# Exact weights alone out of the first stage, late turns by heads, and another order

## The chip, the core and the metric

The kernel runs on one NeuronCore of a Trainium2 chip. The metric is the device time of one execution in microseconds (us). Before the change the median of three runs is 785.89 us (785.5 to 787.57). Five engines run side by side, each through its own list of instructions: TensorE (PE in the rows) multiplies, VectorE (DVE) and ScalarE (ACT) do elementwise work, GpSimd (POOL) adds integers, SyncE (SP) issues transfers. An instruction starts when the one ahead of it on its engine is through and the semaphores of its operands allow it.

## The reference

```
scores = q_c @ k_c.T / 8           # 8 batches x 8 heads, chunks of 64 tokens, width 64
attn = exp(scores - max) ; attn = attn / (sum(attn) + 1e-09)
x = attn @ v_c                     # as 4608 tokens x 512
h = x @ w_in                       # 512 x 2048, float64 words
g = s * relu(h)**2 + b
out = g @ w_out                    # 2048 x 512, float64 words
```

## The kernel before

Every product of two fp32 matrices is made of three TensorE products: each operand is split into a high part (a cast on ScalarE) and a low part (the difference, on VectorE), and h·h, h·l and l·h are added up in PSUM. All large matmuls have 512 columns.

Tokens go in blocks of 512 and more. The *first stage* (tokens 0 to 511) is plain: its `up` products (L657), relu, square, split of g into `g_hi` (L674) and `g_lo` (L678), and `down` products (L632). Meanwhile it makes the weights. They come as 64-bit words in 16 "pairs" of tiles, k = 0 to 15, and each pair goes through a chain: `load` on SP, `tail` (L176) and `scale` (L172) on ScalarE, `shift` (L182) and `sign` (L184) on VectorE, `add` (L190) on GpSimd, `hi` (L194) on ScalarE, `lo` (L198) on VectorE. Attention for the tokens runs beside it in groups one, two, ... of 256 tokens: `scores`, `peak` (L373), `sub` (L378), `exp`, `sum` (L387), `normz` (L390, L391), `norm` (L394), then P is transposed on TensorE (`transposes`, L404) and copied by ScalarE (`copies`, L417), or, for groups seven and later, on VectorE (`turn`, L412), and then `values` (L424) and `x_out` (L440).

From *block 0* on, the MLP works with seven products in place of eight for each 2x2 set of tiles (p1 to p7, L713), for which sums of weight quarters are needed: `s_add` (four additions or subtractions, L233), `s_hi` (L238), `s_lo` (L241) for w_in, and `OutSums` for w_out in block 0's second half (the down steps d0 to d31). The high and low parts of all weights and sums are stored in DRAM scratch (w_in, w_out, w_sum) and read again, 1 MB at a time, by `stream.load` (L330, the "ring" steps) into the three buffers of the pool `raw`.

The order of all instructions is written out by hand. The string ORDER names the steps; they are run in that order, and each engine's list follows from it, since the pool of tiles and the scheduler move nothing (`manual_schedule`). Before the change ORDER ends with block 0's first half; block 0's second half is in `direct` and in hooks, the later blocks in loops of their own.

```
for name in ORDER.split():
    named[name.split("/")[0]]()
block.direct()
```

GpSimd does nothing but the adds of the pairs and ends with the last of them, at 116.5 us.

Of the kernel before, what the change touches and what calls it, by code (L numbers as in the profile page):

```python
# [19 lines left out]
one.load_qk0 one.load_qk1 load0b one.load_v load0a two.load_qk0 two.load_qk1 load1 two.load_v three.load_qk one.scores0 one.peak0  # L20
s_and_b sb one.sub0 one.exp0 one.scores1 keep_busy7 one.peak1 one.sum0 three.load_v one.sub1 one.normz0 one.norm0
one.exp1 four.load_v tail0b one.transposes0 keep_busy3 one.sum1 one.normz1 one.copies0 one.norm1 tail0a scale0a load2
one.transposes1 four.load_qk shift0a scale0b two.scores0 keep_busy8 one.copies1 sign0a shift0b add0a two.peak0 two.sub0
hi0a sign0b two.scores1 two.exp0 lo0a add0b two.peak1 one.values0 keep_busy7 two.sum0 one.x_hi0 two.sub1
load3 hi0b one.x_lo0 two.exp1 lo0b one.values1 keep_busy4 tail1 two.normz0 in0 two.sum1 one.x_hi1
scale1 two.norm0 two.normz1 two.transposes0 keep_busy2 two.norm1 one.x_lo1 shift1 two.copies0 two.values0 sign1 two.transposes1
two.x_hi0 two.copies1 add1 two.x_lo0 up1a scale2 tail2 two.values1 shift2 up0a hi1 sign2
two.x_hi1 three.scores lo1 add2 two.x_lo1 in1 three.peak scale3 up1b tail3 three.sub up0b
open_o load4 relu1 shift3 hi2 up3 sign3 relu0 three.exp lo2 square0 square1
add3 three.sum out0 up2 g_hi0 relu3 g_hi1 load5 square3 three.normz tail4 g_lo0  # L30
g_hi3 three.norm down0 scale4 g_lo1 hi3 shift4 relu2 g_lo3 three.transposes sign4 square2
g_hi2 down1 load6 lo3 tail5 scale5 add4 g_lo2 in2 three.copies up4 shift5
hi4 sign5 tail6 load7 four.scores lo4 relu4 scale6 add5 up5 out1 four.peak
square4 five.load_qk g_hi4 four.sub hi5 shift6 down2 load8 g_lo4 relu5 sign6 tail7
scale7 lo5 three.values four.exp add6 in3 square5 up6 four.sum three.x_out g_hi5 shift7
hi6 g_lo5 down3 sign7 relu6 square6 four.normz g_hi6 load9 add7 tail8 g_lo6
up7 scale8 four.norm hi7 lo7 four.transposes relu7 square7 load10 shift8 up8 scale9
in4 lo6 four.copies sign8 g_hi7 tail9 down4 shift9 out2 add8 g_lo7 relu8
square8 tail10 up9 g_hi8 sign9 load11 hi8 g_lo8 add9 scale10 down5 relu9
square9 g_hi9 shift10 hi9 lo8 five.scores sign10 out3 down6 scale11 load12 five.peak  # L40
six.load_qk add10 tail11 g_lo9 five.sub down7 hi10 shift11 lo9 five.exp sign11 in5
four.values lo10 tail12 up11 add11 five.sum scale12 load13 five.load_v out4 four.x_out five.normz
hi11 up10 shift12 five.norm x21.hi relu11 sign12 x11.hi down8 x21.lo relu10 square11
# [6 lines left out]
s_add0 ring2 s_hi1 lo15 s_hi0 s_add7 relu15 six.transposes out7 square15 down13 g_hi15  # L50
s_add5 six.copies s_lo0 six.values s_lo1 s_keep0 g_lo15 down14 six.x_out s_add6 s_keep1 x22.hi
xt1.add_dve seven.scores x22.lo xt1.hi seven.load_v down15 xt3.add_dve eight.load_qk xt1.lo xt3.hi xt2.add_dve p1.0
st2 st1 xt3.lo xt2.hi p2.0 seven.peak u1.0 st0 p1.1 xt2.lo st3 c11.0
p5.0 u1.1 xt4.add_dve relux.0 p6.1 s_add3 xt4.hi p6.0 u2.1 seven.sub p7.1 xt4.lo
ring3 u2.0 seven.exp s_add2 p7.0 u3.1 p2.1 seven.sum u3.0 c22.0 p4.0 seven.normz
c11.1 p3.0 s_add4 c21.0 relux.1 sqx.0 p4.1 ring4 c12.0 seven.norm s_hi2 p1.2
c21.1 s_lo2 split0.hi p5.1 seven.turn0 s_keep2 u1.2 sqx.1 p6.2 reluy.0 c22.1 p2.2
split0.lo u2.2 ring5 sqy.0 seven.turn1 p3.1 split1.hi p7.2 c11.2 s_hi3 seven.turn2 relux.2
p1.3 ring6 u3.2 c12.1 p4.2 seven.turn3 reluy.1 p5.2 u1.3 sqy.1 s_lo3 seven.values
eight.scores ring7 c21.2 c22.2 sqx.2 s_keep3 split1.lo p3.2 seven.x_out eight.peak eight.load_v nine.load_qk  # L60
p2.3 eight.sub s_hi4 c12.2 p6.3 eight.exp c11.3 reluy.2 eight.sum p5.3 ring8 relux.3
s_lo4 sqy.2 p1.4 eight.normz u2.3 s_keep4 eight.norm p2.4 u1.4 eight.turn0 p6.4 p7.3
c11.4 u2.4 eight.turn1 relux.4 p7.4 u3.3 c22.3 p4.3 u3.4 eight.turn2 p3.3 ring9
c21.3 sqx.3 eight.turn3 p1.5 s_hi5 c12.3 p4.4 ring10 s_lo5 u1.5 reluy.3 p5.4
s_keep5 c21.4 sqy.3 eight.values nine.scores c22.4 sqx.4 p3.4 eight.x_out nine.load_v nine.peak p6.5
nine.sub s_hi6 ring11 c12.4 p2.5 nine.exp s_lo6 reluy.4 p1.6 c11.5 ten.load_qk s_keep6
u2.5 nine.sum relux.5 p7.5 sqy.4 nine.normz u1.6 p5.5 nine.norm u3.5 nine.turn0 p4.5
ring12 p2.6 c21.5 c22.5 sqx.5 nine.turn1 p3.5 c11.6 p1.7 s_hi7 c12.5 nine.turn2
relux.6 p6.6 u1.7 reluy.5 p5.6 s_lo7 ring13 u2.6 sqy.5 nine.turn3 p7.6 s_keep7
p6.7 u3.6 c22.6 ring14 p4.6 u2.7 p3.6 c21.6 sqx.6 p2.7 c12.6 reluy.6  # L70
p7.7 c11.7 sqy.6 ring15 p5.7 relux.7 u3.7 d0 c22.7 p3.7 p4.7 c12.7
reluy.7 ring16 c21.7 sqy.7 sqx.7
# [4 lines left out]
def local_attention_then_squared_relu_mlp(ctx: ExitStack, tc, qkv, w, s, b, out):  # L77
# [219 lines left out]
    class Stream:  # L297


        def __init__(self, blocks):  # L300
# [8 lines left out]
            whole = (slice(None),)  # L309
            self.left = [[(t, whole)] for t in (once + direct * 2 + (once + parts) * (blocks - 1))]  # L310
            self.start = [0] + [len(once) + 2 * len(direct) + n * (len(once) + len(parts)) for n in range(blocks - 1)]
            kept = {n for (p, name), n in units.items() if not name.startswith("s")}
            for n in range(7 * NP // 4):
                mine = [u for u in range(4) if 4 * n + u in kept]
                runs = [(u, next(v for v in range(u, 5) if v not in mine)) for u in mine if u - 1 not in mine]
                self.left[n] = [(w_in[:, n, :, u:v], (slice(None), slice(None), slice(u, v))) for u, v in runs]
# [912 lines left out]
```

## Time and profile before

| | |
|---|---|
| median of three runs | 785.89 us |
| span of the profiled execution, first to last instruction | 783.3 us |
| TensorE busy | 770.7 us (98%) |
| VectorE busy | 615.1 us (79%), 891 instructions |
| ScalarE busy | 470.3 us (60%) |
| GpSimd busy | 48.8 us (6%), 23 instructions |
| HBM read, written | 159.38 MB, 44.04 MB |
| TensorE's granted clock over the span | full |

The page gives the profiled execution by its span; the runs' times count what lies around it too, and their median is 2.6 us above it. TensorE sets the time where it never waits, which is read from its idle time by stretch and not from the 98%. The other engines' shares are means over stages that differ: VectorE is all but full up to 150 us and has time to spare behind.

### The profile page before, as it was taken

What the parts mean: (1) busy time and instruction counts of PE and PEld (TensorE: products, weight loads), DVE (VectorE), ACT (ScalarE), POOL (GpSimd) and SP (SyncE); (2) the same over time, 40 slices, a digit from 0 to 9 for tenths busy, and PEclk for the clock granted to TensorE, in tenths of its full rate; (3) what the DMA queues carried; (4) which work ended last, traced back from release to release, by engine and by line L of the source; (5) the groups of instructions that cost most, each with busy time, mean ns of one, the idle gap of its engine ahead of it and who ended that gap; (6) DMA issues with size and microseconds to landing.
All of it is one profiled execution on the core that took longest, in us unless ns stands there. A gap on an engine that the chain in (4) does not pass through costs nothing.

```text
span 783.3 us, 13870 instructions
## 1 busy us (share of the span) xinstructions
PE 770.7 (98%) x5584; PEld 637.7 (81%) x5584; DVE 615.1 (79%) x891; ACT 470.3 (60%) x645; POOL 48.8 (6%) x23
## 2 busy tenths in 40 slices
PE   6899999999999999999999999999999999999998
PEld 5788888888888888888888888888888888888886
DVE  6989899998479986888899858888998723348773
ACT  4899876867643433566864635666846346575442
POOL 1453440000000000000000000000000000000000
PEclk9999999999999999999999999999999999999999
DMA  9999999678568999966466587665565778876653
GB/s 356 354 357 340 365 304 322 224 243 282 178 216 295 327 343 320 335 246 241 165 213 223 181 311 282 253 264 203 168 230 177 242 263 294 300 266 215 209 193 136
DMA packets 79844, 204.33 MB, mean 261 GB/s; under 512 B 5796, under 2 KB 39076, under 8 KB 68516
## 3 DMA queue, kind: packets, MB, share of 16 engines
q1 hardware_dynamic: 79488, 203.18, 74.6%
q8 instruction: 44, 0.72, 0.4%
q10 hardware_dynamic: 292, 0.26, 0.1%
q14 instruction: 20, 0.16, 0.1%
HBM read 159.38 MB, written 44.04 MB: 260 GB/s over the span
## 4 chain that ended last, share of the span: by engine, by line
PE 91%; DMA 4%; ACT 2%; DVE 1%; issue 1%; SPq 0%; ACTq 0%
PE ps_h L713 22%; PE ps_h L933 17%; PE ps_o L713 17%; PE ps_x L933 8%; PE ps_x L632 8%; PE ps_o L632 5%; PE ps_o L933 4%; PE ps_h L657 3%; PE ps_h L632 3%; DMA raw<-in_w_dram 3%; PE ps_a L368 2%; PE ps_x L424 1%; DMA t<-in_qkv_dram 1%; PE ps_a L424 1%; ACT raw L176 1%; ACT t L172 1%
## 5 line engine op out<-in xcount | busy, mean ns | idle before, releaser
L713 PE MATMUL ps_h<-t,raw 128*128 128x512 f32 x672 | 167.3, 391 | 0.0
L713 PEld LDWEIGHTS ps_h<-t,raw 128*128 128x128 f32 x672 | 125.4, 188 | 26.5 <-ACT u L723 0.2
L933 PE MATMUL ps_h<-t,raw 128*128 128x512 f32 (+1 forms) x588 | 142.4, 385 | 0.0
L907 DVE TENSOR_TENSOR t<-t 128x512 fp32r<-128x512 f32 (+1 forms) x120 | 105.2, 896 | 33.3 <-ACT t L905 33.2
L933 PEld LDWEIGHTS ps_h<-t,raw 128*128 128x128 f32 x588 | 108.8, 188 | 22.2
L732 DVE TENSOR_TENSOR t<-ps_o,u 128x512 f32<-128x512 f32 x96 | 66.0, 689 | 75.3 <-PE ps_o L713 69.9
L713 PE MATMUL ps_o<-t,raw 128*128 128x512 f32 x480 | 121.8, 389 | 0.0
L713 PEld LDWEIGHTS ps_o<-t,raw 128*128 128x128 f32 x480 | 90.1, 188 | 18.8
L723 ACT COPY u<-ps_h 128x512 f32<-128x512 f32 x96 | 56.1, 586 | 69.6 <-PE ps_h L713 68.6
L905 ACT CAST t<-t 128x512 fp32r<-128x512 f32 (+1 forms) x120 | 87.3, 788 | 2.8 <-PE ps_h L933 1.9
L412 DVE STREAM_TRANSPOSE pT<-p 32x256 f32<-32x256 f32 x192 | 83.7, 436 | 3.2
L933 PE MATMUL ps_x<-t,raw 128*128 128x512 f32 x288 | 73.1, 389 | 0.0
L776 ACT ACTIVATE t<-t 128x1024 f32<-128x1024 f32 x64 | 67.1, 1052 | 0.2
L933 PEld LDWEIGHTS ps_x<-t,raw 128*128 128x128 f32 x288 | 54.1, 188 | 11.2
L772 ACT ACTIVATE t<-t 128x512 f32<-128x512 f32 (+1 forms) x64 | 54.1, 846 | 10.2 <-DVE t L732 9.7
L190 POOL TENSOR_TENSOR t<-t,raw 128x1024 int32<-128x1024 int32 (+1 forms) x17 | 48.1, 2827 | 67.1 <-DVE t L184 46.4
L632 PE MATMUL ps_x<-t,raw 128*128 128x512 f32 x192 | 48.8, 390 | 0.0
L657 PE MATMUL ps_h<-x,t 128*128 128x512 f32 (+1 forms) x216 | 47.2, 371 | 1.7 <-DVE x L551 1.6
L937 ACT ACTIVATE u<-ps_h,shift,sb 128x512 f32<-128x512 f32 x18 | 13.1, 781 | 58.2 <-PE ps_h L933 58.2
L657 PEld LDWEIGHTS ps_h<-x,t 128*128 128x128 f32 x216 | 36.9, 188 | 8.9 <-DVE x L551 1.8
L632 PEld LDWEIGHTS ps_x<-t,raw 128*128 128x128 f32 x192 | 36.0, 188 | 7.5
L933 PE MATMUL ps_o<-t,raw 128*128 128x512 f32 x144 | 36.5, 389 | 0.0
(133 smaller groups left out, 1010.9 us busy)
## 6 DMA issues: line engine op xcount, KB each, us to landing
raw<-w_in SPq DMA_DIRECT2D x42, 1024.0 KB, 5.9
raw<-w_out SPq DMA_DIRECT2D x34, 1024.0 KB, 5.1
raw<-w_sum SPq DMA_DIRECT2D x24, 1024.0 KB, 5.1
raw<-in_w_dram SPq DMA_DIRECT2D x15, 1024.0 KB, 7.9
qk<-in_qkv_dram SPq DMA_DIRECT2D x15, 1024.0 KB, 7.8
w_out<-t SPq DMA_DIRECT2D x16, 512.0 KB, 6.8
w_sum<-t SPq DMA_DIRECT2D x16, 512.0 KB, 9.3
v<-in_qkv_dram SPq DMA_DIRECT2D x15, 512.0 KB, 4.6
```

Of the source, the lines that this page charges most:

```text
L190: nc.gpsimd.tensor_tensor(out=i, in0=i, in1=low.bitcast(I32), op=ALU.add)
L412: nc.vector.transpose(out=self.pT[k].rearrange("p i a t -> p (i a) t")[:, :, t], in_=p[t, :, k])
L632: nc.tensor.matmul(out=self.ps[m], lhsT=x, rhs=y, start=(j == 0 and i == 0), stop=(j == stop and i == 2))
L657: nc.tensor.matmul(out=self.ps[j][:, cols], lhsT=w[:, c, :], rhs=x[:, c, :], start=(c == 0 and i == 0), stop=(c == NHP - 1 and i == 2))
L713: nc.tensor.matmul(out=ps, lhsT=w[:, e, :], rhs=y[:, e, :], start=start and e + i == 0, stop=e + i == 3, skip_group_check=not start)
L723: nc.scalar.copy(out=u, in_=self.a[p])
L732: nc.vector.tensor_tensor(out=self.tile(p, h)[:, e, :], in0=ps, in1=u, op=ALU.add)
L772: nc.scalar.activation(out=t, in_=t, func=AF.Relu)
L776: nc.scalar.activation(out=t, in_=t, func=AF.Square)
L905: nc.scalar.copy(out=hi, in_=f)
L907: nc.vector.tensor_tensor(out=lo, in0=f, in1=hi.bitcast(F32), op=ALU.subtract)
L933: nc.tensor.matmul(out=self.acc[name][m][:, cols], lhsT=x, rhs=y[:, cols], start=new and q == 0, stop=q == 2, skip_group_check=not new)
```

## The change

The first stage no longer stores the high and low parts of the weights, but the exact weights of w_out alone (`f_out`, 0.5 MB for a pair of tiles). Block 0 makes the parts anew: a cast on ScalarE (`rh`, `oh`, after: L223) and a subtraction on VectorE (`rl`, `ol`, L226), into buffers of the pool `raw`, and stores them from there (`in`, `ok`) for the later blocks. The weights w_in stay in SBUF for it; those of w_out are read again from f_out (`fo`). The exact w_out for the sums need not be added up from the parts where f_out is at hand (`given`).

```
+    class Again:
+        def load(self):
+            self.f = slot()
+            nc.sync.dma_start(out=self.f.rearrange("p j f -> p (j f)"), in_=f_out[:, self.p])
+        def hi(self):
+            f = self.f if self.source is None else whole[self.source]
...
+            self.tile = raw.tile([P, 4 * DM], F32R, name="raw")
...
+            nc.scalar.copy(out=self.h, in_=f)
+        def lo(self):
+            nc.vector.tensor_tensor(out=self.l, in0=self.f, in1=self.h.bitcast(F32), op=ALU.subtract)
...
-    def keep_out(p):
-        for i, t in enumerate(words[2 * p, 1]):
...
-            nc.sync.dma_start(out=w_out[:, p, i], in_=t)
+    def keep_f(p):
+        nc.sync.dma_start(out=f_out[:, p], in_=whole[2 * p, 1].rearrange("p j f -> p (j f)"))
...
-            if self.n == 0 and name.startswith("s"):
-                return sums[p].unit(name)
+            if self.n == 0:
+                return (sums if name.startswith("s") else again_in)[p].unit(name)
...
-            return stream.tiles[self.at + 7 * NP // 4 + k]
+            return again_out[k].tile if k < NP else stream.tiles[k - NP]
```

Groups seven and later lay their scores out by heads (the host orders q and k for it), so that P is turned by one transpose of 128x1024 in blocks of 32 by 32 and four of 32x512 that swap the blocks off the diagonal, where there were sixteen of 32x256. In `normz` a constant tile is added in place of a constant.

```
-            nc.vector.tensor_scalar_add(out=self.z, in0=self.z, scalar1=1e-9)
+            nc.vector.tensor_tensor(out=self.z, in0=self.z, in1=tiny, op=ALU.add)
...
+        def turn(self):
+            self.pT = att.tile([P, 2, 2 * G, 32], F32, name="pT")
+            p = self.p.rearrange("p g h (b k) -> p b (g h) k", b=2)
+            nc.vector.transpose(out=self.pT, in_=p)
+
+        def swap(self, blocks):
...
+                rows, cols = (slice(64 * c + 32 * b, 64 * c + 32 * b + 32) for b in (1 - k, k))
+                nc.vector.transpose(out=self.pT[cols, 1 - k], in_=p[rows, k])
```

ORDER is written anew up to the end of block 0, its second half included (`direct` is gone). A line of it before and now:

```
-load15 out5 tail14 seven.load_qk six.sub up12 relu13 square13 shift14 ring0 six.exp s_add1
+shift13 lo11 tail13 six.scores sign13 up13 s_add1 lo12 scale14 add13 six.peak load15 out5 tail14 seven.load_qk six.sub
```

By engine: TensorE has the same 4395 matmuls, and the scores of group ten no longer stand next to the values of group nine. VectorE has 772 instructions for 891 (192 transposes out, 60 in; 16 subtractions in, 4 sums out). ScalarE has 16 casts more. SP has 342 transfers for 360.

The first place is on VectorE, late in the first stage. L182 and L184 are shift and sign of a pair, L198 is its lo; L233 (after: L258) are the four additions of s_add1; L373, L378 (L395, L400) are peak and sub of group six. Before:

```order
L184 SCALAR_TENSOR_TENSOR t<-raw,t 128x1024
L198 TENSOR_TENSOR t<-t 128x1024
L373 TENSOR_REDUCE m<-ps_a 128x16
L378 TENSOR_TENSOR t<-ps_a,m 128x2x8x64
L182 TENSOR_SCALAR t<-t 128x1024
L233 TENSOR_TENSOR t<-t 128x256 x4
L184 SCALAR_TENSOR_TENSOR t<-raw,t 128x1024
L198 TENSOR_TENSOR t<-t 128x1024
```

and after:

```order
L184 SCALAR_TENSOR_TENSOR t<-raw,t 128x1024
L258 TENSOR_TENSOR t<-t 128x256 x4
L198 TENSOR_TENSOR t<-t 128x1024
L395 TENSOR_REDUCE m<-ps_a 128x16
L400 TENSOR_TENSOR t<-ps_a,m 128x2x8x64
L182 TENSOR_SCALAR t<-t 128x1024
L184 SCALAR_TENSOR_TENSOR t<-raw,t 128x1024
L198 TENSOR_TENSOR t<-t 128x1024
```

The four additions stood between shift and sign of pair 14; they now stand right behind the sign of pair 13, which is what GpSimd's add of that pair waits for. Shift and sign of pair 14 are now adjacent.

The second place is VectorE's list from the last sign (pair 15) on. L678 (after: L721) is g_lo, the eight L233 (L258) are s_add5 and s_add7, L241 (L266) are s_lo, L226 is rl. The last L198 is lo15. Before:

```order
L184 SCALAR_TENSOR_TENSOR t<-raw,t 128x1024
L198 TENSOR_TENSOR t<-t 128x1024
L678 TENSOR_TENSOR t<-ps_h,t 128x512
L233 TENSOR_TENSOR t<-t 128x256 x4
L198 TENSOR_TENSOR t<-t 128x1024
L233 TENSOR_TENSOR t<-t 128x256 x8
L241 TENSOR_TENSOR x<-t,x 128x1024 x2
```

and after:

```order
L184 SCALAR_TENSOR_TENSOR t<-raw,t 128x1024
L198 TENSOR_TENSOR t<-t 128x1024
L258 TENSOR_TENSOR t<-t 128x256 x4
L721 TENSOR_TENSOR t<-ps_h,t 128x512
L258 TENSOR_TENSOR t<-t 128x256 x8
L266 TENSOR_TENSOR x<-t,x 128x1024
L226 TENSOR_TENSOR raw<-t,raw 128x1024
L266 TENSOR_TENSOR x<-t,x 128x1024
L198 TENSOR_TENSOR t<-t 128x1024
L258 TENSOR_TENSOR t<-t 128x256 x4
L721 TENSOR_TENSOR t<-ps_h,t 128x512
```

lo15 has moved behind the sums, and rl0 has come in.

The third place is SP's queue at the start of block 1, whose first weights are the loads raw<-w_in (L330; after: L349); L295 (L323) are stores of sums of w_out, L637 (L680) of block 0's first outputs. Before:

```order
L330 DMA raw<-w_in 128x2048
L295 DMA w_sum<-t 128x1024 x2
L330 DMA raw<-w_in 128x2048 x2
L637 DMA plain<-o 128x512 x4
L354 DMA v<-in_qkv_dram 128x1024
L330 DMA raw<-w_in 128x2048
```

and after:

```order
L323 DMA w_sum<-t 128x1024 x2
L368 DMA qk<-in_qkv_dram 128x2048
L349 DMA raw<-w_in 128x2048 x3
L323 DMA w_sum<-t 128x1024 x4
L680 DMA plain<-o 128x512 x4
L373 DMA v<-in_qkv_dram 128x1024
L349 DMA raw<-w_in 128x2048
```

Three of the loads now stand in a row. Four stores of sums stand between the third and the fourth; before, two stood between the first and the second.

## Rows read from the trace of the kernel before

**Rows 1.** windows: us, busy us (x instructions) by engine, PEclk, DMA share

```profile
39.00:783.00 744.00, 740.70 (x5114) 611.08 (x5112) 583.84 (x842) 444.94 (x609) 35.97 (x12) 1.00 0.74 256
```

**Rows 2.** timeline of PE: start us, us, line, x count

```profile
120.90 1.52 PE L632 MATMUL ps_o<-t 128*128 128x512 f32 x6
122.35 1.16 PE L424 MATMUL ps_a<-pT,v 64*64 64x64 f32 x64
123.44 1.66 PE L632 MATMUL ps_x<-t 128*128 128x512 f32 x6
...
130.34 1.52 PE L713 MATMUL ps_h<-t,raw 128*128 128x512 f32 x6
131.70 1.52 PE L713 MATMUL ps_o<-t,raw 128*128 128x512 f32 x6
```

**Rows 3.** timeline of POOL, 60 to 120 us

```profile
61.33 2.45 POOL L190 TENSOR_TENSOR t<-t,raw 128x1024 int32<-128x1024 int32 x1 [2.86 <-ACT ps_h L669]
...
99.90 3.22 POOL L190 TENSOR_TENSOR t<-t,raw 128x1024 int32<-128x1024 int32 x1 [5.46 <-DVE t L184]
...
113.26 3.21 POOL L190 TENSOR_TENSOR t<-t,raw 128x1024 int32<-128x1024 int32 x1 [3.42 <-DVE t L184]
```

**Rows 4.** timeline of DVE, 30 to 124 us

```profile
37.41 1.18 DVE L390 TENSOR_SCALAR z<-z 128x16 f32<-128x16 f32 x1
...
62.60 2.27 DVE L394 TENSOR_TENSOR t<-t,z 128x1024 f32<-128x1024 f32 x1
...
99.58 1.22 DVE L198 TENSOR_TENSOR t<-t 128x1024 fp32r<-128x1024 f32 x1
...
103.71 1.55 DVE L233 TENSOR_TENSOR t<-t 128x256 f32<-128x256 f32 x4
...
111.82 1.22 DVE L184 SCALAR_TENSOR_TENSOR t<-raw,t 128x1024 uint32<-128x1024 uint32 x1
...
115.90 1.99 DVE L233 TENSOR_TENSOR t<-t 128x256 f32<-128x256 f32 x4
117.81 1.22 DVE L198 TENSOR_TENSOR t<-t 128x1024 fp32r<-128x1024 f32 x1
```

**Rows 5.** timeline of ACT, 84 to 124 us

```profile
85.85 1.16 ACT L176 ACTIVATE raw<-raw 128x1024 int32<-128x1024 uint32 x1 [2.54 <-DMA raw<-in_w_dram]
...
104.39 1.03 ACT L194 CAST t<-t 128x1024 fp32r<-128x1024 f32 x1
...
116.50 1.05 ACT L194 CAST t<-t 128x1024 fp32r<-128x1024 f32 x1 [1.24 <-POOL t L190]
117.46 1.99 ACT L238 CAST x<-t 128x1024 fp32r<-128x1024 f32 x2
...
121.09 1.08 ACT L417 COPY pT<-ps_a 128x512 f32<-128x512 f32 x2
```

**Rows 6.** windows, columns as in rows 1

```profile
123.00:150.00 27.00, 27.00 (x210) 21.77 (x203) 26.82 (x41) 18.80 (x29) 0.00 (x0) 1.00 0.76 257
300.00:330.00 30.00, 30.00 (x317) 25.19 (x316) 20.43 (x33) 14.45 (x23) 0.00 (x0) 1.00 0.91 322
```

**Rows 7.** timeline of SP's queue, 270 to 325 us

```profile
303.01 3.52 SPq L637 DMA_DIRECT2D plain<-o  x4
...
310.59 0.32 SPq L330 DMA_DIRECT2D raw<-w_in  x1
```

**Rows 8.** DMA issues, 270 to 330 us: KB each, median us to landing

```profile
raw<-w_in SPq DMA_DIRECT2D x7, 1024.0 KB, 9.0
```

**Rows 9.** lines by form: busy us, mean ns | idle us

```profile
L412 DVE STREAM_TRANSPOSE pT<-p 32x256 f32<-32x256 f32 x192 | 83.7, 436 | 3.2
...
L907 DVE TENSOR_TENSOR t<-t 128x1024 fp32r<-128x1024 f32 x48 | 58.2, 1218 | 15.0 <-ACT t L905 14.9
...
L907 DVE TENSOR_TENSOR t<-t 128x512 fp32r<-128x512 f32 x72 | 47.0, 682 | 18.3 <-ACT t L905 18.3
```

More of the change, by code (lines that the diff above doesn't have):

```diff
@@ L19 @@
 ORDER = """
[L20 to L43, printed above, removed]
@@ L50 @@
[L50 to L72, printed above, removed]
+one.load_qk0 keep_busy7 one.scores0 one.peak0 one.sub0 one.load_qk1 load0b load0a one.load_v two.load_qk0 two.load_qk1
+two.load_v load1 three.load_qk s_and_b one.scores1 one.peak1 sb one.sub1 load2 four.load_v three.load_v tail0b
@@ new lines @@
+two.transposes1 hi0a lo0a add1 up1a scale2 two.copies1 two.x_lo0 two.values1 two.x_hi1 shift2 up0a hi1 tail2 two.x_lo1
+sign2 three.scores lo1 add2 three.peak up1b up0b tail3 three.sub open_o load4 relu1 scale3 shift3 hi2 up3 sign3 relu0
+three.exp lo2 three.sum square0 square1 add3 out0 up2 g_hi0 g_hi1 load5 three.normz relu3 g_lo0 three.norm relu2
+square3 scale4 g_lo1 shift4 sign4 square2 tail4 hi3 g_hi2 g_hi3 g_lo3 down0 three.transposes down1 load6 lo3 tail5
+scale5 add4 g_lo2 three.copies up4 shift5 hi4 sign5 tail6 load7 four.scores lo4 relu4 square4 g_hi4 scale6 add5 up5
@@ new lines @@
+out1 four.peak load8 five.load_qk four.sub hi5 shift6 down2 g_lo4 relu5 sign6 lo5 three.values four.exp add6 square5
+tail7 scale7 up6 four.sum three.x_out hi6 g_hi5 shift7 down3 sign7 relu6 four.normz g_lo5 load9 add7 tail8 square6
+g_hi6 g_lo6 up7 scale8 four.norm hi7 four.transposes relu7 scale9 square7 g_hi7 load10 shift8 lo7 up8 lo6 four.copies
+sign8 tail9 relu8 down4 shift9 out2 add8 g_lo7 square8 tail10 up9 g_hi8 sign9 load11 hi8 g_lo8 add9 scale10
+five.scores down5 relu9 square9 g_hi9 shift10 hi9 lo8 sign10 load12 out3 down6 scale11 five.peak six.load_qk add10
@@ new lines @@
+tail11 hi10 g_lo9 five.sub down7 shift11 lo9 five.exp sign11 four.values lo10 tail12 up11 add11 five.sum four.x_out
+scale12 load13 five.load_v load14 out4 five.normz hi11 up10 shift12 five.norm x21.hi relu11 x21.lo sign12 x11.hi down8
+square11 relu10 add12 g_hi11 square10 g_hi10 five.transposes g_lo11 scale13 g_lo10 down9 five.copies x11.lo hi12
+shift13 lo11 tail13 six.scores sign13 up13 s_add1 lo12 scale14 add13 six.peak load15 out5 tail14 seven.load_qk six.sub
+up12 relu13 square13 shift14 sign14 six.exp hi13 down10 relu12 g_hi13 lo13 square12 tail15 add14 g_lo13 five.values
@@ new lines @@
+g_hi12 six.sum scale15 down11 g_lo12 hi14 five.x_out six.normz shift15 six.load_v six.norm up14 sign15 lo14 up15 add15
+relu14 square14 g_hi14 s_add0 g_lo14 hi15 down12 s_hi1 rh0 s_add5 s_hi0 s_add7 relu15 six.transposes out7 square15
+down13 six.copies g_hi15 s_lo1 rl0 s_lo0 lo15 rh1 six.values s_add6 g_lo15 rl1 in1 out6 in0 s_keep0 down14 six.x_out
+xt1.add_dve s_keep1 x22.hi seven.scores x22.lo xt1.hi seven.load_v down15 xt3.add_dve eight.load_qk st1 st2 seven.peak
+xt2.add_dve xt1.lo p1.0 u1.0 xt3.hi xt3.lo st3 p2.0 xt2.hi p1.1 u1.1 xt2.lo c11.0 relux.0 p5.0 xt4.add_dve p6.1 u2.1
@@ new lines @@
+xt4.hi p6.0 st0 u2.0 seven.sub s_add3 p7.1 xt4.lo seven.exp s_add2 p7.0 u3.1 u3.0 p4.0 p2.1 c22.0 seven.sum rh2 rl2
+c11.1 seven.normz p3.0 in2 s_add4 c21.0 sqx.0 split0.hi s_hi2 p1.2 u1.2 relux.1 p4.1 seven.norm c21.1 s_lo2 c12.0 p5.1
+s_keep2 sqx.1 p6.2 reluy.0 c22.1 seven.turn p2.2 split0.lo u2.2 rh3 rl3 split1.hi sqy.0 p7.2 p3.1 c11.2 s_hi3
+seven.swap1 seven.swap0 relux.2 p1.3 u3.2 c12.1 p5.2 reluy.1 p4.2 c21.2 u1.3 sqy.1 s_lo3 eight.scores seven.values
+c22.2 sqx.2 seven.x_out rh4 s_keep3 in3 split1.lo p3.2 eight.peak eight.load_v nine.load_qk p2.3 c12.2 eight.sub s_hi4
@@ new lines @@
+rl4 eight.exp c11.3 reluy.2 eight.sum p5.3 relux.3 s_lo4 sqy.2 p1.4 p6.3 eight.normz u2.3 s_keep4 u1.4 rh5 p2.4 p6.4
+p7.3 c11.4 u2.4 relux.4 p7.4 u3.3 p4.3 c21.3 sqx.3 rl5 in5 in4 c22.3 u3.4 eight.norm eight.turn eight.swap0
+eight.swap1 p5.4 p3.3 p1.5 rh6 s_hi5 c22.4 c12.3 p4.4 s_lo5 reluy.3 nine.scores fo1 rl6 in6 s_keep5 sqy.3 eight.values
+c21.4 u1.5 sqx.4 p3.4 eight.x_out nine.peak nine.sub p6.5 s_hi6 c12.4 p2.5 nine.exp s_lo6 reluy.4 p2.6 p1.6 c11.5
+ten.load_qk nine.load_v s_keep6 u2.5 nine.sum nine.normz nine.norm nine.turn p7.5 sqy.4 rh7 relux.5 p5.5 u3.5 c22.5
@@ L143, in local_attention_then_squared_relu_mlp @@
     pairs.append(((NJ - 2, 1), (NJ - 1, 1)))
-    weights, exact, words = {}, {}, {}
+    weights, exact, whole = {}, {}, {}
     class Pair:
@@ L308, in __init__ @@
             parts += [w_out[:, 4 * n:4 * n + 4, :, 3].rearrange("p n i c -> p (n i) c") for n in range(NP // 4)]
[L309 to L316, printed above, removed]
+            self.left = direct + (once + parts) * (blocks - 1)
+            self.start = [0] + [len(direct) + n * (len(once) + len(parts)) for n in range(blocks - 1)]
             self.tiles = []
@@ L367, in scores @@
                 qk = self.qk[i]
-                nc.tensor.matmul(out=self.ps[cols, c, i * NHP + hp, :], lhsT=qk[rows, 0, h, :], rhs=qk[rows, 1, h, :],
+                at = 2 * hp + c if self.late else h
+                (tile, half) = (rows, h % 2) if self.late else (cols, c)
+                k = cols if self.late else rows
+                nc.tensor.matmul(out=self.ps[tile, half, i * NHP + hp, :], lhsT=qk[k, 0, at, :], rhs=qk[k, 1, at, :],
                                  start=True, stop=True)
@@ L1214 @@
     qk = np.stack([qT, kT], axis=2)
+    late = (tokens(a)[12:].reshape(-1, 2, P // 2, H // 2, 2, D).transpose(0, 4, 5, 3, 1, 2).reshape(-1, P, DM) for a in (q, k))
+    qk[12:] = np.stack(list(late), axis=2)
     qkv = np.concatenate([qk[0::2], qk[1::2], tokens(v).reshape(-1, 2, P, DM).transpose(0, 2, 1, 3)], axis=2)
```

172 lines of the change are left out of this document (99 added, 73 removed).

## The prediction

> **What bounds the kernel now.** I read the table of windows first, then the timelines of each engine over the end of the first stage, then SP's over the start of block 1, and last the grouped rows. The windows show that from 39 us on TensorE is busy 740.70 of 744 us at full clock [rows 1]. The change keeps all 4395 matmuls, so it can gain only in the 39 us ahead, and by 3.3 us at most behind them; it loses wherever it makes TensorE wait. The question is therefore what stands close behind TensorE. The timeline of TensorE answers it for one place: six.values (L424) starts at 122.35 us [rows 2], and its operand, six.copies (L417), is made on ScalarE from 121.09 to 122.17 [rows 5]. So 0.2 us are to spare there, and everything that feeds this chain later moves the end of the kernel.
>
> That chain goes back to VectorE and GpSimd. A GpSimd add (L190) takes 2.45 us alone, as at 61.33 [rows 3]; started while a VectorE subtraction runs, it takes 3.2: L198 from 99.58 to 100.80 and the add from 99.90 to 103.12 [rows 3, 4], so it waited for the subtraction and then ran 2.32. Seen from the other side, L394 at 62.60 took 2.27 with an add running until 63.78, where L198 of the same width takes 1.22 [rows 3, 4]. The reader should see a lock: who comes second waits for the whole of the other. The Trainium skill says so in "SBUF — State Buffer", section "SBUF: two separate sides": a VectorE instruction with two SBUF inputs and a GpSimd instruction take a shared port pair exclusively. The trace agrees, with those 2.27 us; it also speaks against the new order, which puts more such instructions behind the start of an add. Each add starts about 0.2 us behind the end of its sign step (L184): 113.04 and 113.26 [rows 3, 4].
>
> **The change part by part.** Times are in the frame of the profiled execution before.
>
> *Head.* Loads, scores and the first pairs are in another order, and normz adds a tile to z (two SBUF inputs) where it added a constant. In the trace the constant's instruction was blocked: 1.18 us for 16 columns, at 37.41 [rows 4], and behind it stands the subtraction of g_lo0 that TensorE's first down step needs. I walked the new order by hand: each instruction behind the one ahead of it on its engine and behind its operands, with the duration of its row. By that TensorE comes to that step 1 to 1.6 us earlier and waits for the same add and the same subtraction: 0. Ends: -1.7 (all of the earlier start is kept) and +0.3. By that rule of the Trainium skill the new form is blocked like the old, which gives 0; if a 128x16 addition were too small to be blocked, -1.0. No row shows a small one.
>
> *Sums of pair 1.* Before, the four additions of s_add1 (L233) stood between shift and sign and took 1.55 us, from 103.71 on [rows 4]. Now they stand right behind the sign step of pair 13. The first, 0.4, runs; then the add of pair 13 takes the lock for 2.32, and the second waits: +2.25. Ends: 0 (VectorE's next instruction keeps the lock, and GpSimd waits for all four) and 2.3.
>
> *lo13.* With those 1.55 us gone from between shift and sign, the sign step of pair 14 ends some 1.8 us behind the subtraction ahead of them (0.68 and 1.22, less overlap). The cast hi13 came between 104.39 and 105.42 [rows 5], about 2.2 behind that subtraction's end at 103.2. So the add of pair 14 goes ahead of lo13 (L198), which is blocked for 2.25; if the cast wins by a hair, 0. I take the block.
>
> *Fewer stores.* The first stage stores 8 x 0.5 MB of exact weights in place of 16 x 0.5 MB to w_out and 48 x 128 KB to w_in: 4 MB for 14. ScalarE waited 2.54 us for a load at 85.85 [rows 5]. Loads that come sooner give back up to that; by the walk 1.7 reaches VectorE. Ends 0 and 2.5. So the sign step of pair 15 is 2.25 + 2.25 - 1.7 = 2.8 late.
>
> *ScalarE behind pair 15.* From the cast at 116.50 to the copies at 121.09 [rows 5] stands one more cast, rh0 (0.95, as from 116.50 to 117.46), and g_hi15 has moved out (0.48): +0.47. The copies are 3.3 late; less the 0.2 to spare, up to 0.3 more if GpSimd starts behind a subtraction: six.values waits 3.4. Ends 0 and 4.3.
>
> *lo15.* Before it ran at 117.81, ahead of the sums s_add5 and s_add7. Now it stands behind twelve additions, two lows of sums and the new subtraction rl0, and s_add0 ahead of it starts inside the add of pair 15, which blocks it (before, only the first addition touched that add's end: 1.99 for the four at 115.90 instead of 1.55 [rows 4]). Counted from that add's end: 0.3 until the blocked addition ends (116.47 and 116.76), 0.8 for two more, 0.6 for g_lo14, 3.1 for eight additions (at 0.39) and four instructions of 1.15 make 9.4, with a short wait for a cast 9.6. TensorE is through six.values 1.3 behind the copies, which come 5.7 + 0.5 behind the add, and wants lo15 in the third matmul of down14, 0.4 on: 7.9. +1.7; ends 0 and 2.5.
>
> *Start of block 0.* VectorE is busy 26.82 of the 27 us from 123 to 150 [rows 6], before it gets rl0, rl1 and rl2 (1.2 each, as L907's 128x1024 [rows 9]) in return for four shorter additions of exact sums later. Block 0's first products have to wait for the tokens' parts that stand behind them: +1.2; ends 0 and 3.4 (three of them, less overlap). The scores of group ten no longer stand beside the values of nine. A lone run of 64x64 matmuls costs TensorE 0.23 us at its edges: 1.45 from 120.90 to 122.35 and 1.50 behind it, against 1.36 for six [rows 2]; two more edges make +0.2 to +0.4, taken as 0.4.
>
> *Turns.* 192 transposes of 32x256 at 436 ns [rows 9] become 12 of 128x1024 and 48 of 32x512. No row has these shapes. By width, as L907's subtractions go (1218 ns at 1024, 682 at 512 [rows 9]), they cost 12 x 1.2 + 48 x 0.7 = 48 us in place of 83.7. If an element costs what it costs now per column they take 12 x 1.74 + 48 x 0.87 = 63, if turning many blocks at once is slower still, more than 84. They lie under TensorE, which has no wait there now: 0; ends 0 and +2.
>
> *Start of block 1.* Between the third and the fourth load of the block's first weights SP now has four stores of w_sum (2 MB; before, two stood ahead of the second load) and, as before, the plain stores (L637, which took SP from 303.01 on [rows 7]). From 300 to 330 us the queues are busy 0.91 at 322 GB/s [rows 6]; the fourth load was issued at 310.59 [rows 7] and one takes 9.0 from issue to landing [rows 8], so it came about when it was needed. 1 MB more ahead of it is 3 us at that rate, of which most stands ahead of less urgent loads: +0.7; ends 0 and +4.
>
> **The sum.** 0 + 3.4 + 1.7 + 1.2 + 0.4 + 0 + 0.7 = +7.4 on the span of 783.3: 790.7. The median of the runs stands 2.59 above the span, so 793.3.
>
> **The rivals.**
> *No change or little, by GpSimd waiting.* If VectorE's next instruction keeps the lock, GpSimd waits 1.1 longer for the sums, VectorE loses nothing, and lo13's block is not reached since the relief of 1.7 covers the rest. What remains is the edge (0.4) and some of block 0: 783.3 + 0 to 2.5 + 2.6 = 786 to 788.4. For it: no row shows two such VectorE instructions in a row with an add waiting. Against it: when the add ended at 116.47, VectorE's addition ended 0.29 later, so the lock does change hands between instructions.
> *Faster.* The head keeps 1.7 (the small addition isn't blocked, the first down step starts earlier) and the loads' relief covers the rest: with the last waits of 0.4 behind 39 us gone and the edge hidden, 783.3 - 1.7 - 0.4 + 2.6 = 783.8, and a little below 783.5 if the tail behind the last matmul is shorter. It decides if g_lo0 is ready 1 us earlier. Against it: the add of pair 3 ends when it did.
> *Slower still, by loads.* If the 2 MB of stores hold the fourth load for their whole 4 us, TensorE waits at 320 us: 793.3 + 3.3 = 796.6. For it: the busy queues [rows 6]; against it: the stores may come when the loads ahead of them are through, and the half of block 0's loads of w_out that are gone leave room.
> *Turns dearer than thought*: +2 on the forecast if VectorE becomes the bound in block 0: 795.3.
>
> **How the numbers follow.** Forecast (790 to 796) 0.57; GpSimd waiting 0.14; faster 0.12; loads 0.10; turns 0.07. The likeliest alone is 793.3, with 790 to 796 for itself. With the others, 785 to 798 leaves 2 in 10 out at most. This kernel's runs spread by 0.26%, so 0.3% (2.4 us) is what can be told from no change: below 783.5 faster, above 788.3 slower. Faster: half of that rival, 0.06; same: its other half and 0.11 of GpSimd waiting, 0.17; slower: the rest, 0.77.
>
> **What would show it.** Right: in the profile after, the second addition of s_add1 takes over 2 us with an add of GpSimd beside it; L198 of pair 13 takes over 3; TensorE idles 3 to 4 us ahead of six.values with ScalarE as releaser, and 1 to 2 ahead of down14 with VectorE. Wrong: these additions at 0.4 and a GpSimd add of over 3.5; no idle time of TensorE from 100 to 150 us; or idle time at 315 to 325 that outweighs it. The forecast falls if the copies of group six end within 1 us of before.

## The result, and the profile after

The changed kernel takes 792.38 us (median of 4 runs, 792.25 to 795.52), the kernel before 786.14 us in the runs beside it (785.5 to 787.57): ratio 1.0080, 95% interval 1.0060 to 1.0101. It is slower by 6.2 us; 793.3 was forecast. The span of the profiled execution went from 783.3 to 790.4 us; 790.7 was forecast.

TensorE's idle time tells where. The rows are its timeline; the last bracket is the idle time ahead and what ended it.

```profile
40.05 1.43 PE L675 MATMUL ps_x<-t 128*128 128x512 f32 x5 [1.34 <-DVE t L721]
...
47.31 2.56 PE L700 MATMUL ps_h<-x,t 128*128 128x512 f32 x10 [0.41 <-DVE t L198]
...
124.95 1.16 PE L467 MATMUL ps_a<-pT,v 64*64 64x64 f32 x64 [1.90 <-ACT pT L459]
126.04 0.74 PE L675 MATMUL ps_x<-t 128*128 128x512 f32 x2
128.38 1.20 PE L675 MATMUL ps_x<-t 128*128 128x512 f32 x4 [1.60 <-DVE t L198]
...
134.81 1.52 PE L756 MATMUL ps_h<-t,raw 128*128 128x512 f32 x6
...
147.01 1.66 PE L756 MATMUL ps_h<-t,raw 128*128 128x512 f32 x6 [0.67 <-ACT u L766]
```

```profile
309.50 1.62 PE L756 MATMUL ps_h<-t,raw 128*128 128x512 f32 x6 [1.13 <-ACT o L679]
```

```profile
302.41 1.52 PE L713 MATMUL ps_h<-t,raw 128*128 128x512 f32 x6
```

The first two fences are of the kernel after, the third is the counterpart, before, of the row at 309.50. Both programs have the same 3084 matmuls of 512 columns, so the k-th of one can be set beside the k-th of the other. The changed kernel is 0.6 us late at 113 us, 4.47 at block 0's first product (134.81, before 130.34 [rows 2]), 5.4 at 190, 5.8 from 233 on, 7.09 at block 1's first product (309.50 and 302.41), and 7.21 from 318 us to the end. Nothing is lost or gained behind that.

| step | forecast | measured |
|---|---|---|
| head, with up4 | 0 | +0.6 |
| six.values | +3.4 | +2.0 |
| lo15, at down14 | +1.7 | +1.9 |
| start of block 0 | +1.2 | +0.9 |
| one more run of 64x64 | +0.4 | +0.4 |
| turns | 0 | 0 |
| start of block 1 | +0.7 | +1.4 |
| span | +7.4 | +7.1 |

VectorE's timeline shows the lock, in answer to [rows 4]:

```profile
38.00 1.16 DVE L428 TENSOR_TENSOR z<-z,tiny 128x16 f32<-128x16 f32 x1
...
97.89 1.21 DVE L184 SCALAR_TENSOR_TENSOR t<-raw,t 128x1024 uint32<-128x1024 uint32 x1
99.03 3.78 DVE L258 TENSOR_TENSOR t<-t 128x256 f32<-128x256 f32 x4
...
108.41 1.23 DVE L198 TENSOR_TENSOR t<-t 128x1024 fp32r<-128x1024 f32 x1 [0.20 <-ACT t L194]
...
114.21 1.22 DVE L184 SCALAR_TENSOR_TENSOR t<-raw,t 128x1024 uint32<-128x1024 uint32 x1
...
116.48 3.77 DVE L258 TENSOR_TENSOR t<-t 128x256 f32<-128x256 f32 x4
...
127.11 1.22 DVE L198 TENSOR_TENSOR t<-t 128x1024 fp32r<-128x1024 f32 x1
```

and GpSimd's, in answer to [rows 3]:

```profile
35.84 3.30 POOL L190 TENSOR_TENSOR t<-t,raw 128x1024 int32<-128x1024 int32 x1 [2.08 <-DVE t L184]
...
99.34 2.73 POOL L190 TENSOR_TENSOR t<-t,raw 128x1024 int32<-128x1024 int32 x1 [4.18 <-ACT t L172]
108.42 3.52 POOL L190 TENSOR_TENSOR t<-t,raw 128x1024 int32<-128x1024 int32 x1 [6.35 <-ACT t L194]
115.66 3.19 POOL L190 TENSOR_TENSOR t<-t,raw 128x1024 int32<-128x1024 int32 x1 [3.72 <-ACT ps_h L712]
```

The four additions of s_add1 take 3.78 us (99.03) where they took 1.55 [rows 4]. VectorE's timeline of that stretch alone gives the second and the third by themselves:

```profile
99.37 0.41 DVE L258 TENSOR_TENSOR t<-t 128x256 f32<-128x256 f32 x1
...
99.70 2.65 DVE L258 TENSOR_TENSOR t<-t 128x256 f32<-128x256 f32 x1
```

The first two ran, the add at 99.34 waited for both and then held the third up: it ended at 102.07, 2.29 behind the second's end at 99.78. The four of s_add0 take 3.77 beside the add at 115.66. At 38.00 the new form of normz, 16 columns with two SBUF inputs, takes 1.16 like the old one's 1.18 [rows 4]; the add at 35.84 ran until 39.14, so a small addition is blocked too. With no add beside it, at 112.03, it takes 0.17. ScalarE's timeline shows what came of s_add1 and s_add0, in answer to [rows 5]:

```profile
107.34 1.03 ACT L194 CAST t<-t 128x1024 fp32r<-128x1024 f32 x1
...
118.87 1.05 ACT L194 CAST t<-t 128x1024 fp32r<-128x1024 f32 x1 [2.65 <-POOL t L190]
...
123.83 1.06 ACT L459 COPY pT<-ps_a 128x512 f32<-128x512 f32 x2
```

The cast behind the last add starts 2.37 us later than before (118.87 and 116.50 [rows 5]) and the copies of group six 2.74 later (123.83 and 121.09).

The turns cost what their width says:

```profile
L454 DVE STREAM_TRANSPOSE pT<-p 32x512 f32<-32x512 f32 x48 | 33.7, 703 | 0.8
...
L447 DVE STREAM_TRANSPOSE pT<-p 128x1024 f32<-128x1024 f32 x12 | 14.9, 1238 | 0.1
```

33.7 and 14.9 us make 48.6 in place of 83.7 [rows 9], all of it under TensorE, where nothing waits for it. VectorE's busy time fell from 615.1 to 596.2 us, and the time is longer.

### The profile page after: what moved, and what is told of

The parts are those of the page before. It is cut to its first block, busy times and chain, and to the rows that moved or that the text cites. A ratio compares the mean times of both kernels' runs of the same rounds, so it can differ in the third digit from the quotient of the medians.

```text
span 790.4 us, 13690 instructions
## 1 busy us (share of the span) xinstructions
PE 773.0 (98%) x5584; PEld 638.3 (81%) x5584; DVE 596.2 (75%) x772; ACT 482.9 (61%) x661; POOL 46.7 (6%) x23
## 4 chain that ended last, share of the span: by engine, by line
PE 86%; DVE 7%; ACT 4%; issue 1%; DMA 1%; POOL 0%; SPq 0%; POOLq 0%; DVEq 0%
PE ps_h L756 22%; PE ps_h L956 17%; PE ps_o L756 17%; PE ps_x L956 8%; PE ps_x L675 6%; PE ps_o L956 4%; PE ps_o L675 3%; PE ps_h L675 3%; PE ps_a L390 2%; PE ps_h L700 1%; DVE t L198 1%; DVE t L258 1%; PE ps_x L467 1%; DVE t L184 1%; DMA raw<-in_w_dram 1%
## 5 line engine op out<-in xcount | busy, mean ns | idle before, releaser
L766 ACT COPY u<-ps_h 128x512 f32<-128x512 f32 x96 | 56.0, 585 | 66.4 <-PE ps_h L756 66.1
L190 POOL TENSOR_TENSOR t<-t,raw 128x1024 int32<-128x1024 int32 (+1 forms) x17 | 46.0, 2707 | 71.5 <-DVE t L184 31.8
L454 DVE STREAM_TRANSPOSE pT<-p 32x512 f32<-32x512 f32 x48 | 33.7, 703 | 0.8
```

Of the source, the lines that this page charges most:

```text
L190: nc.gpsimd.tensor_tensor(out=i, in0=i, in1=low.bitcast(I32), op=ALU.add)
L454: nc.vector.transpose(out=self.pT[cols, 1 - k], in_=p[rows, k])
L766: nc.scalar.copy(out=u, in_=self.a[p])
```

## The experiments

Each is an edit of the changed kernel unless it says otherwise. In the diffs `-` is where a step stood in ORDER and `+` where it stands, with its neighbours; steps not named keep their places. Times are medians beside runs of the kernel before; spans are of the profiled executions. Line numbers differ by a few where lines were added. The kernel before has medians of 786.14 to 787.32 us beside the different groups of runs, so a difference of less than about 1 us between medians of two groups is read from the traces.

### e1: s_add1 back between shift and sign

```
-sign13 up13 s_add1 lo12
+sign13 up13 lo12
...
-shift14 sign14
+shift14 s_add1 sign14
```

> The changed kernel with one step moved: the four additions of s_add1 stand between shift and sign of pair 14 again, as before the change. Theory (GpSimd's add of pair 13 locks VectorE out of them): the four take 1.55 us instead of 3.78, the add of pair 15 ends about 2.2 us earlier than its 118.85, TensorE's wait of 1.90 ahead of six.values goes; the wait for lo15 (1.60) stays within 0.8 to 1.8, since lo15 and TensorE both come 2 us earlier. Time 792.4 - 1.9 = 790.5. Rival (the copies of group six are late by ScalarE's extra cast rh0, and the additions' wait is absorbed): the wait stays at 1.5 to 1.9 and the time at 792.4.

790.26 us (790.09 to 790.89), 2.1 less than the changed kernel; span 788.3. From 330 us on the k-th matmul is 5.09 us late in place of 7.21. VectorE and TensorE:

```profile
103.21 1.55 DVE L258 TENSOR_TENSOR t<-t 128x256 f32<-128x256 f32 x4
```

```profile
125.50 1.20 PE L675 MATMUL ps_x<-t 128*128 128x512 f32 x4 [0.56 <-DVE t L198]
...
144.13 1.65 PE L756 MATMUL ps_h<-t,raw 128*128 128x512 f32 x6 [0.68 <-ACT u L766]
```

```profile
326.23 3.02 PE L756 MATMUL ps_h<-t,raw 128*128 128x512 f32 x12 [1.53 <-DMA raw<-w_in]
```

The four additions take 1.55 again and the wait ahead of six.values is gone, with rh0 still in ScalarE's list. That one place of four short additions cost 2.1 us is shown. A wait for lo15 of 0.56 stays, less than expected. The wait in block 1 has moved from the first load (309.5) to the fourth (326.2): this is the load that the prediction named.

### e2 and e3: lo15 in front, alone and with e1's move

```
-s_add5 s_hi0 s_add7 relu15
+lo15 s_add5 s_hi0 s_add7 relu15
...
-s_lo0 lo15 rh1
+s_lo0 rh1
```

> The changed kernel with one step moved: lo15 stands ahead of s_add5 and s_add7 again. Theory (its 1.60 us wait is VectorE's order alone): the wait ahead of down14 goes, time 792.4 - 1.6 = 790.8. Rival (VectorE has no room left there, so what is put back by 1.15 us is waited for instead): block 0's first products wait 1 to 2 us for the tokens' parts between 134 and 150 us, and the time stays at 791.8 to 792.4.

> The changed kernel with both moves. Theory of two separate waits: -1.9 and -1.6, 788.9. Rival (VectorE is full up to block 0): only the 2.2 us of the lock come back, 790.2 to 790.5, and the rest is waited for in block 0.

e2: 793.24 us (792.44 to 794.47), span 790.4 as without the move. e3: 790.63 (790.11 to 790.94), span 788.1 against e1's 788.3. In e2 the wait at down14 is gone, and TensorE waits in block 0 for the tokens' parts (L636) instead:

```profile
124.86 1.16 PE L467 MATMUL ps_a<-pT,v 64*64 64x64 f32 x64 [1.86 <-ACT pT L459]
...
138.31 1.43 PE L756 MATMUL ps_o<-t,x 128*128 128x512 f32 x5 [0.38 <-DVE t L636]
...
140.58 5.67 PE L756 MATMUL ps_h<-t,x 128*128 128x512 f32 x23 [0.61 <-DVE t L636]
```

The rivals hold: VectorE is full, and what is put in front is taken from what stands behind. So the 1.6 us at lo15 are not a price of lo15's place.

### e4: the kernel before with s_add1 behind the sign of pair 13

```
-sign13 in6 up13 lo12 scale14 add13
+sign13 s_add1 in6 up13 lo12 scale14 add13
...
-ring0 six.exp s_add1
+ring0 six.exp
```

> The kernel before with one step moved: s_add1 directly behind the sign of pair 13, as the change has it. Theory of the lock: its second addition is blocked, the four take 3.7 to 3.8 us, the copies of group six come about 2 us later with 0.2 to spare, TensorE waits 1.8 to 2.1 ahead of six.values, 786.1 + 1.9 = 788.0 (up to 790 if lo13 is blocked as well). Rival (the block is hidden, or VectorE keeps the lock through all four): no wait, 786.1.

789.04 us (788.0 to 790.32, 10 runs), the kernel before 787.32 beside it: 1.0019, interval 1.0007 to 1.0031. One step's place makes the old kernel slower by 1.7 us:

```profile
100.06 3.69 DVE L221 TENSOR_TENSOR t<-t 128x256 f32<-128x256 f32 x4
```

```profile
125.55 1.16 PE L412 MATMUL ps_a<-pT,v 64*64 64x64 f32 x64 [1.75 <-ACT pT L405]
```

3.69 us for the four additions and 1.75 of wait at six.values: the lock and its price, without any other part of the change. By the k-th matmul this execution is 3.2 us behind the profiled one of the kernel before at 130 us: 1.8 of it at six.values and 1.4 ahead, of which 0.7 came at 67 us, well ahead of the moved step. Here VectorE kept the lock longer. The last of the four additions and GpSimd's add:

```profile
101.18 2.56 DVE L221 TENSOR_TENSOR t<-t 128x256 f32<-128x256 f32 x1
```

```profile
100.37 3.08 POOL L178 TENSOR_TENSOR t<-t,raw 128x1024 int32<-128x1024 int32 x1 [5.27 <-DVE t L172]
```

Three additions ran ahead of the add and the fourth was blocked. In both kernels the add starts 0.31 us behind the first addition (100.37 and 100.06, 99.34 and 99.03), so the starts alone don't tell at which addition the lock changes hands; why it differs stays open.

### e5 and e9: idle matmuls against the half clock at the head

TensorE now waits 4.36 us for the first norm (before, idle matmuls filled most of that time), and its clock falls. The windows of the kernel after, columns PE busy (x), PEclk, DMA share, GB/s:

```profile
10.00:12.00 2.00, 1.11 (x8) 0.50 1.03 420
12.00:15.00 3.00, 3.00 (x60) 0.53 1.03 429
```

0.50 is 1.2 GHz. e5 adds `keep_busy16 keep_busy16` behind `one.peak1`, e9 one `keep_busy16`.

> The changed kernel with 32 idle matmuls of 128x128 (their result is used nowhere) behind one.peak1, where TensorE waits 4.36 us and its granted clock then stands at 0.50 to 0.53 from 10 to 15 us. Theory (the head's 0.6 us come from TensorE working at half clock there): the clock stays at 1.00 through 10 to 15 us, the transposes and scores at 10.9 to 14.5 take half as long, g_lo0 comes 0.4 to 0.7 us earlier than 39.37, time 791.8. Rival (VectorE's and GpSimd's list sets g_lo0, whatever TensorE does): g_lo0 within 0.1 us, time 792.4.

> The changed kernel with 16 keep_busy matmuls behind one.peak1 in place of e5's 32, so that they end before the transposes are due (each takes two passes of 0.11 us: 3.6 of the 4.4 us of idle time; e5's took 7.4 and held the transposes up by 3). Theory (the half clock from 10 to 15 us delays two.scores, and everything up to g_lo0 follows it at a fixed distance, as in e5, where 1.3 us stayed 1.3): clock 1.00, group two's first peak at 13.7 to 14.2 instead of 15.42, g_lo0 1.2 to 1.7 us earlier, time 790.7 to 791.2. Rival (loads or the weights' pairs hold the head at its place): g_lo0 less than 0.5 earlier, time 792.0 or more.

e5: 797.13 us (794.41 to 798.02). I had sized it wrongly: each idle matmul takes two passes, the 64 ran for 7.4 us and held the transposes up by 3. Of the head it says only that g_lo0 follows two.scores at a fixed distance (both 1.3 us later). Of the rest of its loss, 2.0 us come where the clock falls again, in the last section, and most of what remains is waits for loads, at 333 and 713 us. e9: the clock stays at full, g_lo0 comes at 38.83 instead of 39.37, and TensorE now waits for group two's load:

```profile
10.00:12.00 2.00, 0.94 (x7) 1.00 1.03 408
12.00:15.00 3.00, 2.38 (x72) 1.00 1.05 434
```

```profile
12.62 0.69 PE L510 MATMUL ps_p<-t 64*64 64x64 f32 x32 [1.63 <-DMA t<-in_qkv_dram]
```

792.39 us (791.95 to 795.06), no less than the changed kernel, though the span is 0.3 shorter. So about half a microsecond of the head is the clock's, not the 1.2 to 1.7 expected (the changed kernel and the five others with its head and no idle matmuls there have g_lo0 at 39.10 to 39.48); behind it the load takes over.

### e6: stores behind loads at the start of block 1

SP's queue after, and from issue to landing of the first load of w_in in block 1, issued at 297.52 (the last number of the second fence):

```profile
292.45 0.90 SPq L323 DMA_DIRECT2D w_sum<-t  x2
293.39 0.43 SPq L368 DMA_DIRECT2D qk<-in_qkv_dram  x1
297.52 11.20 SPq L349 DMA_DIRECT2D raw<-w_in  x3
```

```profile
raw<-w_in SPq DMA_DIRECT2D x1, 1024.0 KB, 11.8
```

```
-ring7 os_store2
+ring7
...
-eleven.load_qk ring8
+eleven.load_qk ring8 os_store2
...
-os_lo4 os_store4 os_store6 o1.store
+os_lo4 o1.store
...
+    for k, p in ((6, 4), (8, 6)):
+        extra[1].setdefault(("a", k), []).append(out_sums[p].store)
```

> The changed kernel with SP's queue altered at the start of block 1: the stores of the sums of pair 2 stand behind the first load of w_in, those of pairs 4 and 6 behind the fourth (inside block 1). Theory (TensorE's wait of 1.13 us at 309.5 is for that load, issued at 297.52 and held up by the stores and qk ahead of it): the load takes 10 us or less instead of 11.8, the wait goes, and none comes up at 326: time 791.2. Rival (the first load takes that long anyway, or the product waits for ScalarE's copies of the outputs): the wait stays above 0.8, 792.2.

791.51 us (790.85 to 793.62), span 788.8: 0.9 less in the median and 1.6 in the span, of which 0.3 at the head, where nothing was altered. The first load takes 8.5 us, and TensorE doesn't wait from 300 to 330 us at all:

```profile
300.00:330.00 30.00, 30.00 (x199) 25.18 (x198) 16.72 (x22) 14.13 (x21) 0.00 (x0) 1.00 0.95 325
```

The k-th matmul is 5.62 us late before block 1 and 5.62 behind it. The wait is the load's; "ACT o L679", which the row at 309.50 names, is only the last of several semaphores.

### e7: two sums later

```
-rh0 s_add5 s_hi0 s_add7 relu15
+rh0 s_hi0 relu15
...
+s_lo4 s_add5
...
+s_lo5 s_add7
```

It has e1's move too.

> The kernel of e1 with s_add5 and s_add7 (eight additions, 3.0 us) taken from in front of lo15 to behind s_lo4 and s_lo5, 40 us later. Theory (VectorE is full from 114 to 150 us; what was given back in e2 and e3 is given back for want of room): lo15's wait of 0.56 goes and so do the waits for tokens' parts in block 0; the one at 144 us for u (0.68, ScalarE) stays. 790.3 - 0.8 = 789.5. Rival (the additions are waited for where they are now): a wait of 1 us or more between 150 and 175, 790.3 or more.

790.16 us (789.26 to 792.41), e1's within the runs' spread. Up to block 0 it does what was expected: no wait from 48 to 143 us. Then:

```profile
143.01 1.66 PE L756 MATMUL ps_h<-t,raw 128*128 128x512 f32 x6 [0.68 <-ACT u L766]
...
189.15 1.66 PE L756 MATMUL ps_o<-t,raw 128*128 128x512 f32 x6 [0.27 <-DVE t L775]
```

```profile
325.99 3.04 PE L756 MATMUL ps_h<-t,raw 128*128 128x512 f32 x12 [1.62 <-DMA raw<-w_in]
```

The k-th matmul is 1.1 us earlier than in e1 at 130 us, 0.6 at 190, and 0.2 behind the fourth load, with 1.62 us of wait for e1's 1.53. It is unclear in the time and clear in the trace.

### e8, e10 and e11: all repairs

e8 is e7 with e5's idle matmuls and e6's stores, `lo3` ahead of `g_lo3`, and `p2.1` ahead of `u3.1`. e10 has one `keep_busy16`. e11 is e10 with `two.load_qk0` ahead of `load0a`, and `s_add5`, `s_add7` behind `c21.3`, `c21.5`.

> The changed kernel with all repairs: e7, e5's idle matmuls, e6's stores, lo3 right behind the sign of pair 4 (0.41 us at up4), and p2.1 ahead of the copies u3.1 and u3.0 (0.68 at 144 us). If the waits found are all there is and independent: 792.4 less 1.9, 1.9, 0.4, 0.9, 1.2 and 0.5 = 785.6, equal to the kernel before. If they aren't, 787 to 789; what is left is then read from TensorE's idle time.

> The kernel of e8 with 16 keep_busy matmuls in place of 32. Theory: the offset of 1.35 us that e8 had from the head on becomes -1.0 to -1.4, the rest as in e8: 787.9 - 2.5 = 785.4, at or below the kernel before by the shared runs. Rival (the head is held by something else): 787 or more.

> The kernel of e10 with two.load_qk0 ahead of load0a (512 KB less ahead of it on SP; in e9 and e10 TensorE waits 1.3 to 1.6 us at 12.5 for that load) and s_add5, s_add7 behind c21.3 and c21.5. Theory (behind the clock that load is what held the head): the wait at 12.5 goes, g_lo0 comes 0.8 to 1.3 us earlier than 38.73, time 786.3 - 1.1 = 785.2, below the kernel before by 0.1 to 0.2%. Rival (pair 0's own load, now later, or VectorE holds the head at its place): less than 0.4 earlier, 786.0 or more.

e8: 787.89 us (787.65 to 788.85; 1.0008 of the kernel before, 0.9992 to 1.0024). e10: 786.26 (785.87 to 786.99; 0.9993, 0.9983 to 1.0004). e11: 786.19 (785.45 to 787.12, 11 runs; 0.9987, 0.9978 to 0.9996), a tenth of a per cent under the kernel before and 6.2 us under the changed one. The traces don't show that tenth: e11's span is 784.3, the 783.3 of the kernel before is shorter, and by the k-th matmul e11 is 1.0 late. In the runs beside it the kernel before has a mean clock of 0.997 to 0.999 in 10 of 15, e11 has 1.0 in all 11, which would fit; that is argued, not shown. e8 lies where the waits were expected if they aren't independent; at 40 us it is 1.7 us late by the head, which the idle matmuls hold up as in e5. e10 lies between its two expectations. In e10 the k-th matmul is 0.7 us early at 130 us, 0.5 late at 190 and 0.9 late at 300. So the waits found are nearly all there is; the additional run of 64x64 matmuls (0.4) and short waits in block 0 remain.

e11 didn't do at the head what it was to: TensorE doesn't wait at 12.5 any more, but g_lo0 comes at 39.01, 0.3 later than in e10. The idle matmuls took 5.50 us there (first fence) and 3.84 in e10 (second):

```profile
6.94 5.50 PE L126 MATMUL ps_h<-t 128*128 128x128 f32 x32
```

```profile
6.50 3.84 PE L126 MATMUL ps_h<-t 128*128 128x128 f32 x32
```

In e11 they came about 0.21 us apart up to 10 us and 0.11 behind it, in e10 0.11 to 0.12 nearly throughout: half and full rate, though the page's clock says 1.00 in both. So they ran until 12.4 us in e11 and put the transposes off from 10.55 to 12.28, and the load ahead was not tested. In the changed kernel, e5, e9, e10 and e11 g_lo0 starts 24.7 to 24.8 us behind the second half of two.scores, so the head is held by what holds these scores; whether that is the load or pair 0 once the clock is full stays open.

## Why the prediction was right

**The sum.** That the span came out within 0.3 us is in part luck. The steps missed by +0.6, -1.4, +0.2, -0.3 and +0.7 (table above), and these cancel. The median's further 0.6 is the distance from span to median, taken as 2.59 and here 2.0. Two of the signs that were to show the forecast right did not come: lo13 did not take over 3 us, and TensorE idled 1.9 us ahead of six.values, not 3 to 4. The direction, the lock and the waits at six.values and lo15 were right by their mechanism.

**The lock.** s_add1's block was put at +2.25 and measured 2.23 (3.78 less 1.55); e1 and e4 show it from both sides, in 2.1 and 1.7 us of the time. The rule of the Trainium skill that stood beside it ("SBUF — State Buffer", section "SBUF: two separate sides") holds in these runs to the width of 16 columns (1.16 us at 38.00). The forecast had the second addition blocked; it was the third, and in e4 the fourth. So the rival in which VectorE keeps the lock is half right: VectorE kept it for one or two more additions, but not for all four, and the price is the same while one of them is left.

**lo13.** This step failed: 2.25 was forecast, 0.2 measured. The cast ended at 108.37 (107.34 and 1.03), L198 started at 108.41 after 0.20 of idle time, and the add of pair 14, at 108.42, waited for it and took 3.52. The prediction had called it close, and it went the other way, by hundredths of a microsecond. The cast ended 2.02 us behind the end of the subtraction ahead of the shift (105.12 and 1.23), where 2.2 was counted. Against that the relief by fewer stores was smaller too: the add of pair 13 was issued 0.56 us earlier than before (99.34 and 99.90), at the end of a head that is 0.6 late, so about 1.2 where 1.7 was forecast. (ScalarE waits for no load from 40 to 120 us, where it waited 6.9 before; that the stores alone did this was not tested.) The sign of pair 15 is 2.4 late (114.21 and 111.82) for 2.8 forecast: 2.23 and 0.2, less 0.56, and 0.5 in short gaps of VectorE's list between 103 and 113 us that the prediction didn't have. The 2 us too many at lo13 are thus nearly made up by a late head, a smaller relief and these gaps; that is luck.

**six.values and lo15.** 2.0 instead of 3.4 follows from that: 2.4 at the cast, 0.37 more behind it for rh0 (forecast 0.47), less what was to spare and what TensorE itself was late. lo15's 1.6 us of wait (1.9 by the k-th matmul) came as worked out (1.7): lo15 ended 9.5 us behind the end of the last add (9.6 forecast), and TensorE wanted it at 7.9. But e2 and e3 show that the step was read too narrowly: the wait belongs to VectorE's list as a whole, not to lo15's place.

**The head.** "0" was 0.6. The prediction saw that TensorE would wait for the same add and subtraction, and not that its new idle time lowers its clock, which delays the add too. e9 gives 0.54 us back.

**Start of block 0.** The 0.9 is near the 1.2, but it is not the wait that was forecast. The one wait there, 0.67 us at 147.01, ends with one of ScalarE's copies u (L766), and it is gone in e8 and e10, where p2.1 stands ahead of two of them (u3.1, u3.0). The tokens' parts were waited for in e2 and e3 alone, where TensorE came to them sooner.

**Block 1.** Right in kind, wrong in the transfer: the first load, not the fourth, was late in the changed kernel; with TensorE 2 us or more earlier (e1, e7) it is the fourth. e6's stores take the first wait away, and e8 and e10, with these stores and e1's move, have neither. The prediction looked at the stores ahead of the fourth load; ahead of the first now stand two stores that stood behind it before. The term was mis-sized, 0.7 for 1.4.

## What to carry to other kernels

Where GpSimd and VectorE read SBUF, look at what stands directly behind the instruction that starts GpSimd: a group of short two-input instructions there loses over 2 us, while beside the add of pair 14 an instruction that reads PSUM (L721 at 109.55) and a reduction (L425 at 110.15) took their usual 0.68 and 1.21. Moving four additions to another place in the list was worth 2 us of 790. When an engine is full, a wait at one of its results is not repaired by moving that result (e2); moving work out of the stretch took the waits there away (e7), though most of the gain was lost again behind it. Less traffic and less busy time gain nothing where TensorE doesn't wait for them; a queue's order decides which load is late.
